# Weight loads moved to SyncE's queue, attention rows of four pairs moved to GpSimd, and a new instruction order, in a fused threshold attention and feed-forward kernel

## The chip, the cores and the metric

The kernel runs on one core of one Trainium2 chip. The core has five engines with instruction queues of their own: TensorE (PE; PEld is its weight load), VectorE (DVE), ScalarE (ACT), GpSimd (POOL) and SyncE (SP). Each works through its queue in order; engines wait for one another through semaphores. DMA transfers are issued by SyncE, ScalarE or GpSimd and carried out by 16 DMA engines that all of them share. The metric is the device time of one execution in microseconds, here the median of several runs.

## What is computed

Threshold attention over 8 batches and 8 heads, 576 tokens, 64 wide; its output, with the heads side by side, is the input of a feed-forward layer with a quick GELU.

```python
scores = scale * np.matmul(q, k.transpose(0, 1, 3, 2))
thresh = np.max(scores, axis=-1, keepdims=True) - tau
scores = np.where(scores >= thresh, scores, -1000000000.0)
scores = scores - np.max(scores, axis=-1, keepdims=True)
attn = np.exp(scores)
attn = attn / (np.sum(attn, axis=-1, keepdims=True) + 1e-09)
attn_out = np.matmul(attn, v).astype(np.float32)
x = np.ascontiguousarray(attn_out.transpose(0, 2, 1, 3)).reshape(B * S, H * D)   # 4608 x 512
h = x @ w_in                                     # 512 x 2048
g = h * (1.0 / (1.0 + np.exp(-1.702 * h)))
out = (g @ w_out).astype(np.float32)             # 2048 x 512
```

q, k and v are 32-bit floats. The two weight matrices come as 64-bit floats, and the kernel makes 32-bit ones of them on the chip.

## The kernel before

**Units of work.** Two heads make a pair: 32 pairs, four in each batch, numbered through. Tokens of the feed-forward part go in 18 blocks of 256 (`BLK`). A block needs all pairs of its tokens' batch.

**Stages.** The four pairs of batch 0 are worked "straight" (functions `straight_...`, lines 640 to 760): scores with queries on the partitions, row maximum on VectorE, threshold and exponential on ScalarE, transposes on TensorE (L699, L700), copies out of PSUM, then the product with v (L740) and the reciprocal sums (L746). All later pairs use transposed scores: `scores` (L531), `keep` (copies on ScalarE, L548), `in_groups` (group maxima and later group sums on VectorE, L554), a fold over the groups, `sub`, `mask`, `exps` and `values` (L767), and `place_x` (L859), which writes the block's input. The first two blocks use plain products: `mm1_0` (L917) and `mm2` (L896). Later blocks use `mm1` (L874) and a Strassen form of the second product, `product` (L1068), which needs sums of weight quarters; these come from `t_minus` (a negation on ScalarE) and `t_plus` (four accumulating DMAs of 1 MB issued by GpSimd, L1028). The last four blocks use a Strassen form of the first product as well (L982).

**Weights.** `load_w` (L455) brings 32 pieces of 128 x 512 numbers, 512 KB each, to staging places: unused quarters of `w_out`'s home and four places in `arena`, twelve in all. GpSimd issues them. `cv_ex`, `cv_frac`, `cv_join` and `cv_end` on VectorE (L463, L481, L488, L495) and `cv_power`, `cv_power2` on ScalarE (L470, L474) turn a piece into 32-bit numbers; `cv_end` frees its place. The first six pieces also wait for `hold` (L522), a one-column copy on GpSimd that reads pair 3's transposed k, so that no weight moves before the q and k of the four straight pairs are in.

**Loads and rows by SyncE.** `load_qk` (L392) and `load_v` (L406 for the straight pairs, L414 for the others) issue four DMAs for each tensor and pair, mostly through SyncE. The row of thresholds of a later pair has to reach all partitions: `row_out` (L604) writes it to DRAM in two DMAs, `row_in` (L613) waits for that and reads it back, broadcast, in two more. The reciprocal sums of pairs 4 and up go the same way by `sums_out` (L826) and `sums_in` (L833). All of these were issued by SyncE, as are the stores of results (L1095, L1098).

**Order.** The kernel is scheduled by hand. `task` enters a piece of work with an engine, an estimated duration, a rank, the pieces it comes after, and buffer places that it takes and gives. `run_in_order` then simulates all engines: whenever an engine is free, it starts the ready task of the lowest rank whose places are free, and the instructions are emitted in that order. So a rank sets which of several ready tasks goes first, and an estimated duration moves everything behind it. The rank of a task is its number (pair, or a line such as `W_RANK` for weights) plus a bias by its function's name from `EARLY` (pairs 0 to 3), `SECOND` (pairs 4 to 7), `LATER` or `CV` (weights). Feed-forward work on TensorE has the rank `LAST`. Two movers stand for DMA: "DMS" for transfers of SyncE, "DMW" for those of GpSimd; each takes its transfers in order, and while both are at work they share the rate by `SHARE`.

Of the kernel before, what the change touches and what calls it, by code (L numbers as in the profile page):

```python
# [10 lines left out]
FP32 = mybir.dt.float32  # L11
I32 = mybir.dt.int32
U32 = mybir.dt.uint32
# [6 lines left out]
P = 128  # L20
# [10 lines left out]
def kernel(  # L31
# [34 lines left out]
    nc = tc.nc  # L66
    B, H, S, D = q.shape
# [45 lines left out]
    flat = [const.tile([P, 32], FP32, name=f"flat{j}") for j in range(2)]  # L113
    flat_s = [const.tile([P, 32], FP32, name=f"flat_s{j}") for j in range(2)]
    gap = const.tile([P, 1], FP32, name="gap")
    stop = const.tile([P, 1], FP32, name="stop")
    eye = const.tile([P, P], FP32, name="eye")
    shift = const.tile([P, 1], FP32, name="shift")
    NQT = -(-S // P)
# [10 lines left out]
    for x in ("P0", "P1", "P2", "PT0", "PT1"):  # L130
        limits[x] = 1

    EARLY = {
        "load_qk": -6.99,
        "load_v": 19.38,
        "prep": -0.3,
        "straight_bias": -37.57,
        "straight_copy": 8.04,
        "straight_copy1": 11.5,
        "straight_exps": 20.62,  # L140
        "straight_mask": -13.68,
        "straight_max": -0.2,
        "straight_place": 8.36,
        "straight_rc": 12.79,
        "straight_scores": -8.82,
        "straight_spread": -20.84,
        "straight_turn": -58.57,
        "straight_values": -0.62,
        "w_sum": 90.41,
    }  # L150
    SECOND = {
        "exps": -8.01,
        "in_groups": 121.89,
        "keep": 8.52,
        "load_qk": -60.94,
        "load_v": 127.47,
        "mask": 92.02,
        "over_halves": -26.23,
        "over_tiles": -53.86,
        "place_x": -40.91,  # L160
        "prep": 109.09,
        "row_in": -38.28,
        "row_out": 19.96,
        "scores_run": -1.49,
        "sub": 24.27,
        "sums_in": 27.21,
        "sums_out": -40.63,
        "turn_rows": -31.38,
        "turn_sums": 97.65,
        "values": 117.99,  # L170
    }
    LATER = {
        "exps": 26.76,
        "in_groups": 140.58,
        "keep": -31.05,
        "load_qk": 105.64,
        "load_v": 65.31,
        "mask": 18.17,
        "over_halves": -22.78,
        "over_tiles": 5.19,  # L180
        "place_x": -61.68,
        "prep": -28.15,
        "row_in": -9.02,
        "row_out": 27.42,
        "scores_run": 19.47,
        "sub": 29.93,
        "sums_in": -9.33,
        "sums_out": 25.19,
        "turn_rows": -36.12,
        "turn_sums": -33.9,  # L190
        "values": -39.61,
        "x_sum": -32.27,
    }
    CV = {
        "cv_end": -7.74,
        "cv_ex": -36.17,
        "cv_frac": 2.14,
        "cv_join": -50.97,
        "cv_power": 117.41,
        "cv_power2": 87.54,  # L200
        "load_w": 4.35,
    }

    LAG = {"PE": 0.26, "DVE": 0.18, "ACT": 0.22, "POOL": 0.18, "SP": 0.1}
# [14 lines left out]
    FIRST, LAST = -9.0, 1000.0  # L219
    MOVERS = ("DMS", "DMW")  # L220

    SHARE = (0.22, 0.6)

    def moved(kind):
        pass
# [217 lines left out]
    def load_w(i):  # L443
        dst, src, c, j = pieces[i]
        dram = src[ts(c, P), ts(j, WC)]
        if not wide:
            nc.gpsimd.dma_start(out=dst[:, c, ts(j, WC)], in_=dram)
            return
        at = staged(i)
        if at in W64:  # L450
            t = arena[:, ts(W64.index(at), 2 * WC)]
        else:
            t = w_out[:, ts(HALVES.index(at), 2), :].rearrange("p a b -> p (a b)")
        t = t.bitcast(U32)
        nc.gpsimd.dma_start(out=t, in_=dram.bitcast(U32), max_dma_last_dim=1024)  # L455
        t = t.rearrange("p (c w) -> p c w", w=2)
        cv[i] = t[:, :, 1], t[:, :, 0], dst[:, c, ts(j, WC)]

# [38 lines left out]
        )  # L497


    held_k = {}  # L500
    mats, sT, stats, mbs, rows, pss = {}, {}, {}, {}, {}, {}

    def prep(n, which):

        dst, raw = home(n, f"qkT{which}"), raws.pop((n, which))
        if which and n < NPAIR:
            tiles = raw.rearrange("p (j k) -> p j k", k=KT)
            for u in range(2):
                nc.vector.transpose(
                    out=dst[:, 0 : 8 * KT].rearrange("p (x u k) -> p x u k", u=2, k=KT)[:, :, u],  # L510
                    in_=tiles[:, 5 * u : 5 * u + 4],
                )
            nc.vector.transpose(out=dst[:, 8 * KT :], in_=tiles[:, 4])
        else:
            nc.vector.transpose(out=dst, in_=raw)
        mats[n, which] = dst
        if which:
            held_k[n] = dst

    def hold(n):  # L520

        nc.gpsimd.tensor_copy(out=stop, in_=held_k[n][:, 0:1])  # L522

    def halves(ap):
        return ap.rearrange("p (c s) -> p c s", c=2)
# [72 lines left out]
        mbs[n] = mb  # L598


    def row_out(n):
        rows[n] = dram.tile([2, S], FP32, name="row", tag="row", bufs=2)
        for c in range(2):
            nc.sync.dma_start(  # L604
                out=rows[n][c : c + 1].rearrange("o (g i) -> (o g) i", i=32),
                in_=flat[1][ds(c * KT, QB)],
            )

    def row_in(n):
        mb = home(n, "mb")  # L610
        row = rows.pop(n)
        for c in range(2):
            nc.sync.dma_start(out=mb[ts(c, KT)], in_=row[c : c + 1].to_broadcast([KT, S]))  # L613
        mbs[n] = mb

    def sub(n, t):
# [206 lines left out]
    def sums_out(n):  # L823
        rcs[n] = dram.tile([2, 2, SH], FP32, name="row_s", tag="row_s", bufs=2)
        for c in range(2):
            nc.sync.dma_start(  # L826
                out=rcs[n][c].rearrange("h (g i) -> (h g) i", i=32), in_=flat_s[1][ds(c * KT, QB)]
            )

    def sums_in(n):  # L830
        rc, row = seat("rc"), rcs.pop(n)
        for h in range(2):
            nc.sync.dma_start(  # L833
                out=rc[ts(h, D)].rearrange("p (c s) -> p c s", c=2),
                in_=row[:, h].unsqueeze(0).to_broadcast([D, 2, SH]),
            )
        rcs[n] = rc
# [307 lines left out]
    BY_DMA = (0, 1, *range(3, NP))  # L1145
    SUMS_BY_DMA = range(4, NP)
    LEAD = 6
    WHOLE = 6

    FFU = 1.727  # L1150
    T_RANK = FIRST

    W_RANK = (-53.35, -5.67, 56.61, 61.89, -5.56, 48.51)
    W_TIME = 1.9
    ready_w, w_loads = [], []
    for i in range(len(pieces)):
        y = 0 if i < NDC else 2 if i < n_in else 4
# [4 lines left out]
            ready_w.append(task("POOL", 1.2, rank, load_w, i, lag=2.5))  # L1162
            continue
        place = (staged(i),)
        a = task("POOL", 0.6, rank, load_w, i, after=w_loads[-1:], take=place)
        w_loads.append(a)
        a = transfer("DMW", W_TIME, a)

        over = [
            ready_w[y] for y in range(i)  # L1170
# [220 lines left out]
        return transfer("DMS", 0.7 if n < NPAIR else 1.1, lv, 1)  # L1391

    HOLD = 3
    S_RANK = (-4.42, -17.19, 4.68)

    def straight(preps):
        order = [(n, t) for n in range(NPAIR) for t in range(2)]
# [5 lines left out]
        for u, (n, t) in enumerate(order):  # L1403
            r = S_RANK[0] * n if t < 2 else S_RANK[1] + S_RANK[2] * n
            whole, H = heads(t) == 2, range(heads(t))
            if t in (0, 2):
                lv = one_v(n, 1.0 + (0.5 * n if t == 0 else 1.6 + 0.6 * n))
            pt, pp = f"PT{u % 2}", f"P{p_of(n, t)}"
            a = task(
                "PE", 1.0 if whole else 0.6, r, straight_scores, n, t, after=preps[n] + chain[0][-1:],  # L1410
                take=("psA",) * heads(t) + (pp,), give=("s_m",) if t == NQT - 1 else (),
            )
            chain[0].append(a)
# [7 lines left out]
            if last_of[p_of(n, t)] == u:  # L1421
                back = ((pp,), ("mb", "rc"), ("s_t", "s_t"))[p_of(n, t)]
            a = task(
                "PE", 1.1 if whole else 0.55, r, straight_turn, n, t, after=es + chain[1][-1:],
                take=("psA", "psM"), give=back,
            )
            chain[1].append(a)
# [10 lines left out]
            new = n == 0 and t % 2 == 0  # L1438
            first = [spread_0[0, t // 2 * 2]] if not new else []
            a = task(  # L1440
                "PE", 1.31 if whole else 0.85, r, straight_values, n, t, after=c + [d, lv],
                give=(pt,) + ((f"v_m{n % 2}",) if t in (1, NQT - 1) else ()),
            )
            spread_0[n, t] = task(
# [10 lines left out]
    SPLIT = (True,)  # L1455
    preps = [load_pair(n, 0.5 * n, [], False) for n in range(NPAIR)]
    tasks[tau_done][5].extend(preps[0])
    h = task("POOL", 0.3, FIRST, hold, HOLD, after=preps[HOLD][1:])
    for a in w_loads[0:6]:
        tasks[a][5].append(h)  # L1460
    straight(preps)
    first_blocks()

    for n in range(NPAIR, NP):
# [3 lines left out]
        r = float(n)  # L1468

        slow = 1.1 if n < 2 * NPAIR else 1.0  # L1470
        behind = [spread[n - 2]] if n >= NPAIR + 2 else preps[-1]
        pq, pk = load_pair(n, r, behind, True)
        lv = one_v(n, r - 1.2)
        mx, copies = [], []

# [50 lines left out]
        )  # L1526
        if n in BY_DMA:
            a = task("DVE", 0.21, r, turn_rows, n, after=[a])
            a = transfer("DMS", 0.3, task("SP", 0.65, r, row_out, n, after=[a]))
            spread[n] = task("SP", 1.1, r, row_in, n, after=[a], take=("mb",))  # L1530
            m = transfer("DMS", 0.7, spread[n], 1, give=("row",))
        else:
            m = task("DVE", 0.78, r, spread_max, n, after=[a], take=("mb",))
        spread.setdefault(n, m)
# [21 lines left out]
        if n not in SUMS_BY_PE:  # L1556
            su = [
                task("DVE", 0.77 if t == NKT else 1.3, r, in_groups, n, t, ALU.add, after=[ws[t]])
                for t in range(NKT + 1)
            ]  # L1560
            a = task("DVE", 0.47, r, over_tiles, n, ALU.add, after=su + [pv], give=back)
            if n in SUMS_BY_DMA:
                a = task("DVE", 1.46, r, turn_sums, n, after=[a], take=("row_s",))
                a = transfer("DMS", 0.3, task("SP", 0.65, r, sums_out, n, after=[a]))
                a = task("SP", 1.2, r, sums_in, n, after=[a], take=("rc",))
                summed[n] = transfer("DMS", 0.7, a, 1, give=("row_s",))
            else:
                a = task("DVE", 1.6, r, one_group, n, after=[a])
        exped[n] = ws + su
# [40 lines left out]
```

## Time and profile before

| | us |
|---|---|
| median of 3 runs | 1312.84 (1311.53 to 1313.91) |
| the profiled execution, its own time | 1317.27 |
| its span, first to last instruction | 1315.5 |
| TensorE busy in the span | 1275.2 |
| VectorE busy | 987.2 |
| ScalarE busy | 675.9 |
| GpSimd busy | 241.8 |
| first `mm1_0` (L917) | at 72.11 |
| first `mm1` (L874), once pairs 4 to 7 are placed | at 283.80 |

DMA by queue, from the page:

```profile
q1 hardware_dynamic: 181456, 63.70, 20.4%
q0 software_dynamic: 8800, 20.97, 6.2%
```

q1 carries what SyncE issues (packets, MB, share of 16 engines over the span), q0 what GpSimd issues: the weights and the four accumulates.

How to read it: in the profile a line such as "L455 POOL" is line 455 of the kernel before on GpSimd; "SPq" is SyncE's queue of DMA issues. A row's duration there is how long the engine took to issue, not the transfer. "A <- B" in the view of waits means that A's engine stood idle until B. The busy time of TensorE has modelled ends, so a busy TensorE is not one at its peak. A stretch's DMA share can exceed 1 by a little, since packets overlap.

### The profile page before, as it was taken

Reading aid. Unit: us, or ns where it says so; the run is one execution under the profiler, and the core shown is the slowest. Engines: PE = TensorE matmul, PEld = TensorE weight load, DVE = VectorE, ACT = ScalarE, POOL = GpSimd, SP = SyncE. Lnnn points to the kernel's source line nnn. Section 1 sums busy time; section 2 is a strip of 40 time slices with the busy share of each in tenths; the row PEclk is TensorE's granted clock in tenths of the full one; section 3 lists DMA queues with packets and bytes.
Section 4 is the critical chain, followed back from the end, with each engine's and each line's share of the span. In section 5 each row is a group of like instructions: output and inputs, shape, how many; then the busy total and the mean of one; then the engine's idle time right before and its main releaser. Section 6 shows DMA issues by size and latency. Waiting matters only on the chain.

```text
span 1315.5 us, 22946 instructions
## 1 busy us (share of the span) xinstructions
PE 1275.2 (97%) x9140; PEld 994.8 (76%) x9140; DVE 987.2 (75%) x1648; ACT 675.9 (51%) x954; POOL 241.8 (18%) x265
## 2 busy tenths in 40 slices
PE   6599999899999999999999999999999999999998
PEld 4466764467887777777778887777777778888887
DVE  6698998998978888788787878777788863652642
ACT  6699965867745544555554555454555540210210
POOL 3001101013131211213021302021112117120120
PEclk9799999999999999999999999999999999999999
DMA  7724346364422222212222222222122110000000
GB/s 170 206 58 142 90 132 125 71 130 80 89 64 71 55 55 69 49 53 56 56 44 71 55 71 55 71 55 67 39 58 54 37 45 9 9 1 29 4 1 32
DMA packets 192730, 86.42 MB, mean 66 GB/s; under 512 B 159856, under 2 KB 173168, under 8 KB 192624
## 3 DMA queue, kind: packets, MB, share of 16 engines
q1 hardware_dynamic: 181456, 63.70, 20.4%
q0 software_dynamic: 8800, 20.97, 6.2%
q8 instruction: 71, 1.16, 0.4%
q10 hardware_dynamic: 2368, 0.30, 0.1%
q14 instruction: 35, 0.29, 0.1%
HBM read 71.04 MB, written 9.70 MB: 61 GB/s over the span
## 4 chain that ended last, share of the span: by engine, by line
PE 79%; DVE 6%; ACT 5%; DMA 4%; issue 3%; SPq 1%; POOL 0%; DVEq 0%; POOLq 0%; ACTq 0%
PE ops L1068 25%; PE hps L874 24%; PE pv L767 9%; PE ps L531 8%; PE ps L982 4%; PE ps L1068 4%; PE ops L982 3%; PE ops L896 2%; DVE arena L618 2%; ACT arena L628 1%; SPq L392 1%; DMA arena<-in_moe_w_in_dram 1%; ACT arena L624 1%; ACT arena L548 1%; DVE part L554 1%
## 5 line engine op out<-in xcount | busy, mean ns | idle before, releaser
L554 DVE TRANSPOSE_TENSOR_REDUCE part<-arena 128x36 f32<-128x1152 f32 (+1 forms) x280 | 338.2, 1234 | 43.8 <-ACT arena L548 24.0
L874 PE MATMUL hps<-xT,w_in 128*128 128x256 f32 x1536 | 336.7, 380 | 0.0
L874 PEld LDWEIGHTS hps<-xT,w_in 128*128 128x128 f32 x1536 | 290.8, 190 | 44.7 <-issue 5.7
L624 ACT ACTIVATE arena<-arena 128x1152 f32<-128x1152 f32 (+1 forms) x140 | 144.3, 1061 | 140.8 <-DVE arena L618 139.9
L1068 PE MATMUL ops<-w_out,arena 128*128 128x256 f32 x896 | 202.5, 380 | 0.9 <-DVE arena L886 0.8
L548 ACT COPY arena<-ps 128x576 f32<-128x576 f32 x252 | 150.4, 644 | 99.5 <-PE ps L531 97.8
L618 DVE TENSOR_TENSOR arena<-arena 128x1152 f32<-128x1152 f32 (+1 forms) x140 | 179.8, 1326 | 14.8 <-DMA arena<-row 14.8
L1068 PEld LDWEIGHTS ops<-w_out,arena 128*128 128x128 f32 x896 | 169.2, 190 | 28.3 <-DVE arena L886 2.7
L628 ACT ACTIVATE arena<-arena,shift,scl 128x1152 f32<-128x1152 f32 (+1 forms) x140 | 170.0, 1246 | 1.2
L1034 POOL TENSOR_TENSOR arena<-arena 128x256 f32<-128x256 f32 x56 | 52.0, 928 | 637.1 <-DVE arena L886 531.3
L531 PE MATMUL ps<-arena 64*64 64x288 f32 x2016 | 151.0, 408 | 6.3 <-ACT arena L548 4.9
L1068 PE MATMUL ops<-arena 128*128 128x256 f32 x672 | 150.6, 380 | 0.0
L883 ACT ACTIVATE th<-hps 128x512 f32<-128x512 f32 x112 | 66.5, 593 | 162.6 <-PE hps L874 153.5
L767 PE MATMUL pv<-arena 64*64 64x288 f32 x2016 | 147.3, 407 | 0.0
L1068 PEld LDWEIGHTS ops<-arena 128*128 128x128 f32 x672 | 127.3, 190 | 19.3 <-issue 2.2
L531 PEld LDWEIGHTS ps<-arena 64*64 64x64 f32 x2016 | 72.7, 133 | 58.1 <-ACT arena L548 16.8
L767 PEld LDWEIGHTS pv<-arena 64*64 64x64 f32 x2016 | 74.6, 134 | 51.2 <-issue 11.3
L1090 DVE SCALAR_TENSOR_TENSOR osb<-ops,osb 128x256 f32<-128x256 f32 x98 | 39.3, 413 | 93.8 <-PE ops L1068 87.5
L886 DVE SCALAR_TENSOR_TENSOR arena<-th,hps 128x512 f32<-128x512 f32 x96 | 64.5, 672 | 45.5 <-ACT th L883 45.3
L917 PE MATMUL hps<-xT,w_in 128*128 128x256 f32 x256 | 60.8, 387 | 3.4 <-DVE arena L923 2.4
L917 PEld LDWEIGHTS hps<-xT,w_in 128*128 128x128 f32 x256 | 46.8, 190 | 16.2 <-DVE arena L923 5.8
L1047 POOL TENSOR_TENSOR arena<-arena 128x512 f32<-128x512 f32 x28 | 38.1, 1363 | 113.1 <-PE ops L1068 113.1
(129 smaller groups left out, 1289.4 us busy)
## 6 DMA issues: line engine op xcount, KB each, us to landing
arena<-in_v_dram SPq DMA_DIRECT2D x112, 144.0 KB
arena<-in_q_dram SPq DMA_DIRECT2D x128, 72.0 KB
out_dram<-osb SPq DMA_DIRECT2D x36, 256.0 KB
arena<-in_k_dram SPq DMA_DIRECT2D x124, 72.0 KB
arena<-row SPq DMA_DIRECT2D x56, 144.0 KB
arena<-row_s SPq DMA_DIRECT2D x56, 144.0 KB
w_out<-in_moe_w_in_dram POOLq DMA_DIRECT2D x12, 512.0 KB, 9.2
arena<-in_moe_w_out_dram POOLq DMA_DIRECT2D x12, 512.0 KB, 5.2
```

The lines of the kernel that those rows point to most:

```text
L531: nc.tensor.matmul(ps[ts(c, KT), h, 0:SH], lhsT=mats[n, 1][ts(h, D), ts(j, KT)], rhs=mats[n, 0][ts(h, D), ts(c, SH)], start=True, stop=True,)
L548: nc.scalar.copy(out=sT[n, t][:, u], in_=pss.pop((n, j))[:, :, 0:SH])
L554: nc.vector.tensor_reduce(out=stats[n, op][:, t * 2 * QB : min(2 * t + 2, NK) * QB], in_=sT[n, t].rearrange("p u h (g d) -> p (u h g) d", ...
L618: nc.vector.tensor_tensor(out=s, in0=s, in1=mbs[n].unsqueeze(1).to_broadcast(list(s.shape)), op=ALU.subtract)
L624: nc.scalar.activation(out=s, in_=s, func=AF.Prelu, alpha=STEEP)
L628: nc.scalar.activation(out=s, in_=s, func=AF.Exp, scale=scl, bias=shift)
L767: nc.tensor.matmul(o[c][ts(h, D), 0:SH], lhsT=left(j, h)[ts(c, KT)], rhs=sT[n, t][ts(c, KT), u, h, :], start=(j == 0), stop=(j == NK - 1),)
L874: nc.tensor.matmul(hidden[j][:, ts(f, BLK)], lhsT=w_in[:, c, ds((f * HF + j) * P, P)], rhs=xTs[blk][:, c, :], start=(c == 0), stop=(c == N ...
L883: nc.scalar.activation(out=ths[j], in_=hidden[j], func=AF.Tanh, scale=GELU_SCALE / 2)
L917: nc.tensor.matmul(hidden[j // 2][:, ts(j % 2, BLK)], lhsT=w_in[:, c, ts(j, P)], rhs=xTs[i][:, c, :], start=(c == 0), stop=(c == NDC - 1),)
L982: nc.tensor.matmul(places[j, x], lhsT=left[:, c, ts(j, P)], rhs=right[:, c, :], start=(c == 0), stop=(c == 1),)
L1068: nc.tensor.matmul(banks[blk][k][:, ts(o, HM)], lhsT=left[:, j, :], rhs=right[:, j, :], start=(j == 0), stop=(j == HF - 1),)
```

## The change

1. `load_w` is issued by SyncE, without the limit of 1024 elements for a DMA's last dimension; its transfers join those of q, k and v in "DMS", as a third kind with a share of its own. Its task is on SyncE at 0.65 us, and a transfer is taken as 1.6 us, not 1.9. `hold`, its tile and its wait are taken out.
2. `row_out`, `row_in`, `sums_out` and `sums_in` go through `row_queue`: GpSimd for the pairs in `ROWS_BY_POOL` (0 to 7; pairs 0 to 3 have no such rows), SyncE for the others. The planner gives them 1.4 times SyncE's cost, the mover "DMW" and a lag of 2.2 us.
3. The loads of q and k of pair 4 and up come after `prep` of the pair before, and after `row_in` of the pair two before only where SyncE issues that.
4. All biases, `W_RANK` and `S_RANK` have new values, and the TensorE tasks of the straight pairs longer estimated durations.

The diff, with the rank tables cut to the entries of loads, rows and a few others:

```diff
-    stop = const.tile([P, 1], FP32, name="stop")
...
     EARLY = {
-        "load_qk": -6.99,
-        "load_v": 19.38,
-        "prep": -0.3,
+        "load_qk": 3.05,
+        "load_v": 82.62,
+        "prep": 362.76,
...
     SECOND = {
-        "in_groups": 121.89,
-        "load_qk": -60.94,
-        "load_v": 127.47,
-        "mask": 92.02,
+        "in_groups": 369.01,
+        "load_qk": -36.91,
+        "load_v": 29.17,
+        "mask": 366.05,
...
     LATER = {
-        "load_qk": 105.64,
-        "load_v": 65.31,
+        "load_qk": 2.64,
+        "load_v": -33.93,
...
     CV = {
-        "cv_power": 117.41,
-        "load_w": 4.35,
+        "cv_power": 390.1,
+        "load_w": 50.41,
...
-    SHARE = (0.22, 0.6)
+    SHARE = (0.15, 0.5, 0.6)
...
-        nc.gpsimd.dma_start(out=t, in_=dram.bitcast(U32), max_dma_last_dim=1024)
+        nc.sync.dma_start(out=t, in_=dram.bitcast(U32))
...
-        if which:
-            held_k[n] = dst
-
-    def hold(n):
-
-        nc.gpsimd.tensor_copy(out=stop, in_=held_k[n][:, 0:1])
...
+    def row_queue(n):
+        return nc.gpsimd if n in ROWS_BY_POOL else nc.sync
+
     def row_out(n):
         rows[n] = dram.tile([2, S], FP32, name="row", tag="row", bufs=2)
         for c in range(2):
-            nc.sync.dma_start(
+            row_queue(n).dma_start(
...
+    ROWS_BY_POOL = range(8)
...
-    W_RANK = (-53.35, -5.67, 56.61, 61.89, -5.56, 48.51)
-    W_TIME = 1.9
+    W_RANK = (-4.5, 72.77, 54.26, 75.15, 32.14, 155.99)
+    W_TIME = 1.6
...
-        a = task("POOL", 0.6, rank, load_w, i, after=w_loads[-1:], take=place)
+        a = task("SP", 0.65, rank, load_w, i, after=w_loads[-1:], take=place)
         w_loads.append(a)
-        a = transfer("DMW", W_TIME, a)
+        a = transfer("DMS", W_TIME, a, 2)
...
-    S_RANK = (-4.42, -17.19, 4.68)
+    S_RANK = (0.4, 5.42, 2.97)
...
-                "PE", 1.0 if whole else 0.6, r, straight_scores, n, t, after=preps[n] + chain[0][-1:],
+                "PE", 1.13 if whole else 0.78, r, straight_scores, n, t, after=preps[n] + chain[0][-1:],
...
-                "PE", 1.1 if whole else 0.55, r, straight_turn, n, t, after=es + chain[1][-1:],
+                "PE", 1.2 if whole else 0.64, r, straight_turn, n, t, after=es + chain[1][-1:],
...
-                "PE", 1.31 if whole else 0.85, r, straight_values, n, t, after=c + [d, lv],
+                "PE", 1.43 if whole else 0.87, r, straight_values, n, t, after=c + [d, lv],
...
-    h = task("POOL", 0.3, FIRST, hold, HOLD, after=preps[HOLD][1:])
-    for a in w_loads[0:6]:
-        tasks[a][5].append(h)
...
-        behind = [spread[n - 2]] if n >= NPAIR + 2 else preps[-1]
+        rq = ("POOL", 1.4, "DMW", 2.2) if n in ROWS_BY_POOL else ("SP", 1.0, "DMS", 1.7)
+        behind = preps[n - 1] + ([spread[n - 2]] if n - 2 >= NPAIR and n - 2 not in ROWS_BY_POOL else [])
         pq, pk = load_pair(n, r, behind, True)
+        preps.append([pq, pk])
...
-            a = transfer("DMS", 0.3, task("SP", 0.65, r, row_out, n, after=[a]))
-            spread[n] = task("SP", 1.1, r, row_in, n, after=[a], take=("mb",))
-            m = transfer("DMS", 0.7, spread[n], 1, give=("row",))
+            a = transfer(rq[2], 0.3, task(rq[0], 0.65 * rq[1], r, row_out, n, after=[a]))
+            spread[n] = task(rq[0], 1.1 * rq[1], r, row_in, n, after=[a], take=("mb",))
+            m = transfer(rq[2], 0.7, spread[n], 1, give=("row",), lag=rq[3])
```

`sums_out` and `sums_in` are edited like `row_out` and `row_in`.

More of the change, by code (lines that the diff above doesn't have):

```diff
@@ L133 @@
     EARLY = {
-        "load_qk": -6.99,
-        "load_v": 19.38,
-        "prep": -0.3,
[L137 to L149, printed above, removed]
+        "load_qk": 3.05,
@@ L150 @@
+        "load_v": 82.62,
+        "prep": 362.76,
+        "straight_bias": -51.59,
+        "straight_copy": -11.87,
+        "straight_copy1": -4.39,
+        "straight_exps": 57.8,
+        "straight_mask": -49.11,
+        "straight_max": -16.77,
+        "straight_place": 30.11,
+        "straight_rc": 32.02,
+        "straight_scores": 63.84,
+        "straight_spread": 5.07,
+        "straight_turn": 64.19,
+        "straight_values": -79.72,
+        "w_sum": 48.82,
     }
     SECOND = {
-        "exps": -8.01,
@@ L153 @@
-        "in_groups": 121.89,
-        "keep": 8.52,
-        "load_qk": -60.94,
-        "load_v": 127.47,
-        "mask": 92.02,
[L158 to L170, printed above, removed]
+        "exps": 53.23,
@@ L171 @@
+        "in_groups": 369.01,
+        "keep": -16.96,
+        "load_qk": -36.91,
+        "load_v": 29.17,
+        "mask": 366.05,
+        "over_halves": 54.1,
+        "over_tiles": 97.84,
+        "place_x": 12.39,
+        "prep": 32.35,
+        "row_in": 55.92,
+        "row_out": 8.7,
+        "scores_run": -21.91,
+        "sub": 17.15,
+        "sums_in": 5.03,
+        "sums_out": -4.82,
+        "turn_rows": 155.43,
+        "turn_sums": 9.77,
+        "values": -69.26,
     }
     LATER = {
-        "exps": 26.76,
@@ L174 @@
-        "in_groups": 140.58,
-        "keep": -31.05,
-        "load_qk": 105.64,
-        "load_v": 65.31,
[L178 to L192, printed above, removed]
+        "exps": 72.34,
@@ new lines @@
+        "in_groups": 363.35,
+        "keep": -33.06,
+        "load_qk": 2.64,
+        "load_v": -33.93,
+        "mask": -0.83,
+        "over_halves": -15.8,
+        "over_tiles": -22.38,
+        "place_x": -59.37,
+        "prep": 51.26,
+        "row_in": 156.1,
+        "row_out": -51.91,
+        "scores_run": 76.83,
+        "sub": 28.89,
+        "sums_in": 32.66,
+        "sums_out": 58.7,
+        "turn_rows": -35.09,
+        "turn_sums": 2.88,
+        "values": -15.13,
+        "x_sum": -24.18,
@@ L193 @@
     }
     CV = {
[L195 to L198, printed above, removed]
-        "cv_power": 117.41,
-        "cv_power2": 87.54,
-        "load_w": 4.35,
+        "cv_end": -5.82,
+        "cv_ex": 67.45,
+        "cv_frac": 58.08,
+        "cv_join": 17.15,
+        "cv_power": 390.1,
+        "cv_power2": 61.04,
+        "load_w": 50.41,
     }
@@ L497, in cv_end @@
         )
-    held_k = {}
     mats, sT, stats, mbs, rows, pss = {}, {}, {}, {}, {}, {}
@@ L612, in row_in @@
         for c in range(2):
-            nc.sync.dma_start(out=mb[ts(c, KT)], in_=row[c : c + 1].to_broadcast([KT, S]))
+            row_queue(n).dma_start(out=mb[ts(c, KT)], in_=row[c : c + 1].to_broadcast([KT, S]))
         mbs[n] = mb
@@ L825, in sums_out @@
         for c in range(2):
-            nc.sync.dma_start(
+            row_queue(n).dma_start(
                 out=rcs[n][c].rearrange("h (g i) -> (h g) i", i=32), in_=flat_s[1][ds(c * KT, QB)]
@@ L832, in sums_in @@
         for h in range(2):
-            nc.sync.dma_start(
+            row_queue(n).dma_start(
                 out=rc[ts(h, D)].rearrange("p (c s) -> p c s", c=2),
@@ L1563 @@
                 a = task("DVE", 1.46, r, turn_sums, n, after=[a], take=("row_s",))
-                a = transfer("DMS", 0.3, task("SP", 0.65, r, sums_out, n, after=[a]))
-                a = task("SP", 1.2, r, sums_in, n, after=[a], take=("rc",))
-                summed[n] = transfer("DMS", 0.7, a, 1, give=("row_s",))
+                a = transfer(rq[2], 0.3, task(rq[0], 0.65 * rq[1], r, sums_out, n, after=[a]))
+                a = task(rq[0], 1.2 * rq[1], r, sums_in, n, after=[a], take=("rc",))
+                summed[n] = transfer(rq[2], 0.7, a, 1, give=("row_s",), lag=rq[3])
             else:
```

## The prediction

> **What bounds the kernel now.** I began with the page: TensorE's share, and the span in 40 slices of 32.9 us.
>
> ```profile
> PE 1275.2 (97%) x9140; PEld 994.8 (76%) x9140; DVE 987.2 (75%) x1648; ACT 675.9 (51%) x954; POOL 241.8 (18%) x265
> ...
> PE   6599999899999999999999999999999999999998
> ...
> ACT  6699965867745544555554555454555540210210
> ```
>
> TensorE is full from the third slice on; only the first two, and a digit of the eighth, have room. The view of busy time by stretch puts numbers on that (stretch, its length, then PE, PEld, DVE, ACT, POOL, granted clock, DMA share, GB/s).
>
> ```profile
> 8.00:48.60 40.60, 32.32 (x284) 21.00 (x284) 34.13 (x92) 33.80 (x64) 10.60 (x15) 0.92 0.90 240
> 48.60:55.70 7.10, 0.00 (x0) 0.00 (x0) 0.00 (x0) 0.00 (x0) 0.75 (x1) 0.60 0.73 172
> 55.70:66.00 10.30, 9.33 (x90) 7.93 (x94) 5.62 (x16) 6.57 (x14) 0.00 (x0) 0.78 0.17 45
> 66.00:165.00 99.00, 95.17 (x953) 68.73 (x946) 87.37 (x187) 96.70 (x178) 9.73 (x13) 1.00 0.36 98
> 165.00:195.00 30.00, 27.61 (x171) 20.47 (x171) 28.40 (x51) 19.58 (x30) 2.25 (x3) 1.00 0.52 140
> 195.00:284.00 89.00, 84.09 (x561) 40.46 (x561) 80.28 (x124) 56.62 (x68) 3.92 (x3) 0.98 0.47 99
> 284.00:1088.00 804.00, 803.66 (x6057) 640.49 (x6056) 647.43 (x982) 433.42 (x546) 158.53 (x163) 1.00 0.26 60
> ```
>
> From 284 us TensorE is busy 803.66 of 804: a fixed amount of matmul work, so whatever the beginning gains or loses, the end gains or loses. From 66 to 165 ScalarE is the bound (96.70 of 99), from 165 to 195 VectorE (28.40 of 30), and TensorE again from 195. Ahead of them lies a hole, 48.6 to 55.7, in which no engine computes. The timeline of SyncE's issues and the waits say why.
>
> ```profile
> 24.25 11.10 SPq L392 DMA_DIRECT2D arena<-in_q_dram  x4
> 35.45 14.80 SPq L392 DMA_DIRECT2D arena<-in_k_dram  x4
> 50.34 22.55 SPq L406 DMA_DIRECT2D arena<-in_v_dram  x16
> PE rest L740 <- DMA arena<-in_v_dram: 10.3, 1, 10.3
> ```
>
> Four loads of q, which took 2.27 us to issue at 8.96, take 11.10 at 24.25, and four of k take 14.80 instead of 2.67. Behind them in SyncE's order stands the next v, issued at 50.34, for which TensorE waits 10.3 us. What slows them is the other queue:
>
> ```profile
> 28.00:32.00 4.00, 3.91 (x44) 2.89 (x44) 3.44 (x10) 3.91 (x9) 1.07 (x2) 1.00 1.02 325
> 32.00:36.00 4.00, 4.00 (x60) 2.79 (x56) 3.97 (x9) 3.97 (x8) 2.01 (x3) 1.00 1.05 340
> ```
>
> The DMA engines are full (share 1.02 to 1.05) with the 512 KB weight pieces that GpSimd issued from 21.6 us on.
>
> **The change, part by part.** (1) *Weights to SyncE.* One queue means that q and k no longer share the engines with weights packet by packet; they take their turn. A piece moves in 0.524 MB / 0.340 MB per us = 1.54 us. No weight issue by SyncE is in the trace: the nearest rows are a 256 KB store, 0.37 us, and one of four q loads, 2.27 / 4 = 0.57. 32 pieces take 12 to 18 us of SyncE, spread over some 180 us. The gain is the hole, 55.7 - 48.6 = 7.1 us, and the low granted clock (0.60 and 0.78 in the two rows) around it: the two batches of twenty L740 matmuls with their L746 last from 55.7 to 60.9, 5.2 us, against 3.9 from 24.0 to 27.8: 1.3. Together 8.4. Two bounds. Another wait may come right behind (gain 0); or everything comes, at most TensorE's whole 10.3 us wait. I take 8.4, because ScalarE and VectorE are idle there too, and ScalarE, the bound of the next 99 us, gets that much more time.
>
> (2) *Weights ahead of the first v.* Ranks order what SyncE has ready: pieces 0 and 1 (-4.5 + 50.41 = 45.9, then 65.2) go ahead of v of pairs 0 and 1 (1.0 + 82.62 = 83.6, 84.1). That costs the first v 2 x (0.37 to 0.57) of issue up to 2 x 1.54 of transfer, 0.7 to 3.1 us. The first L740 (23.97) moves with it; the scores and exps of the next tiles, which ScalarE works on until then, cover it in part. I take 1; without that cover it is 3.1. Taking out `hold` and the GpSimd copy (0.18 us) costs nothing: GpSimd sat idle 18.9 us there.
>
> (3) *Rows of pairs 4 to 7 by GpSimd.* Each pair has two `row_out`, two `row_in`, two `sums_out`, two `sums_in`: 8 DMAs, 32 in all. On GpSimd a DMA takes 0.75 us (the L455 row), so 24 us, against some 14 on SyncE (0.31, 0.49, 0.31 and 0.61 us). GpSimd is idle 27.75 of the 30 us after 165, so the issuing itself is hidden. The latency is not, always: SyncE's first row goes out at 119.64 and `row_in`, which waits for it, starts at 121.47, 1.83 us. GpSimd's tau load landed 3.4 us after issue, and its quickest weight piece in 4.0, less 1.54 of transfer 2.5. So a hop costs +0.6 to +1.6, four hops a pair +2.4 to +6.4. VectorE has other pairs to work on meanwhile (80.28 of 89); exposed is the last pair, whose sums go out at 264.9 and whose chain has to end before the first L874 at 283.8. Against it stands a gain: SyncE's rows stood among other issues, and the chain of waits has these.
>
> ```profile
> 162.15 8.15 DMA row_s<-flat_s
> ...
> 220.23 2.85 DMA row<-flat
> 223.65 7.40 DMA arena<-row
> ```
>
> 7.40 us came beside a 1 MB accumulate and eight q and k loads, and ended in TensorE's wait of 4.91 us on ScalarE at 250. If it goes, the gain is that 4.91; if GpSimd's latency is exposed in full, the cost is 6.4. GpSimd works in order too: a row can now stand behind an accumulate that waits for ScalarE's negation (9.0 us before the one at 207.3), and the accumulate behind a row; that makes the upper end 9.0. I take 0, because VectorE waits only 3.8 us for `row` and 3.0 for `row_s` from 60 to 285.
>
> The Trainium skill has a rule against this part: "SBUF — State Buffer", section "SBUF: two separate sides", says that DMAs issued by GpSimd stall while VectorE holds the port that both share, since their descriptors can't be written; it gives 620 ns alone and 3100 ns overlapped. By the page a hop would be 2.5 us longer and a pair 9.9. In the trace the L455 issue stays at 751 to 782 ns with VectorE nearly full, so the issue shows no such stall; landings of 4.0 to 13.8 us could hide one.
>
> (4) *New ranks, and longer TensorE costs for the planner.* They add no instruction; they change the order on every engine. TensorE's idle time outside the hole and the first 8 us, up to 284, is 8.28 (8 to 48.6) + 0.97 + 3.83 + 2.39 + 4.91, less 3.2 (its 10.3 less the 7.1 inside the hole): 17.2. At best all of that goes, at worst a second hole of 10.3 opens. I take 0, by the nearest row: ScalarE at 96.70 of 99 says that this idle time is mostly TensorE waiting for a full engine, which no order removes. The low priority of `prep` (362.76) and of `in_groups` (369.01) costs nothing as long as VectorE has gaps early (34.13 busy of 40.6). From 284 on, order moves nothing: TensorE is full.
>
> The sum: -8.4 + 1 + 0 + 0 = -7.4. The profiled execution took 1317.27 (span 1315.5 and 1.8 around it), so 1309.9 for it; it lies 4.4 above the median of the runs, 1312.84, so 1305.4 for the median: 1305.
>
> **Rivals.** *A: a v load that waits holds the weights* (slower). SyncE works in order. In the trace it stands for TensorE to free a v seat: L406 on L746 three times, 24.2 us, the longest 17.0; L414 on L740 27.6 us at once. Meanwhile GpSimd went on issuing weights (96.34 to 108.10, 130.88, 132.08, 156.47 to 159.28). After the change these are behind it, wherever the real order runs later than the planned one. One w_in piece held 17.0 us holds the first product as long: 1312.8 + 17.0 - 8.4 = 1321. It decides from a hold of 8.4 us on. Against it: the planner lets SyncE take a v only when its seat is free in its own time, and other pieces are in hand.
>
> *B: the hole moves.* The bytes are the same. If the v of pair 2 queues behind twelve pieces, 12 x 1.54 = 18.5 us of transfer from about 22 to 40 and SyncE is held as before, nothing is gained: 1313. For it: q, k, v and weights fill the engines from 24 to 48. Against: ranks put v of pairs 2 and 3 (84.6, 85.1) ahead of piece 3 (103.9) and later ones, and TensorE needed it only at 45.4. The Trainium skill's "DMA: Bandwidth & Descriptors", section "Issuing engines are not separate DMA queues", is on B's side: all issuers interleave on the same 16 engines and only sequencer time is saved. The trace differs: 11.10 against 2.27 us is what sharing did to q.
>
> *C: GpSimd's latency comes to lie on the chain.* If the beginning ends 8.4 earlier, pair 7's slack (its sums landed near 270.5, mm1 at 283.8: 13) is only 5; with hops at the longest lone landing, 6.08 - 1.54 = 4.5, +2.7 each and +10.8 a pair, in pair 7 and, through SyncE's queue order, once more in pair 6 on the way to 231: -8.4 + 1 + (10.8 - 5) + 4.5 = +2.9, 1316. Against it: VectorE has other work at each hop. The Trainium skill's rule in part 3 speaks for C.
>
> **How the numbers follow.** Forecast 0.55, A 0.20, B 0.13, C 0.12. A measurement tells 0.2%, 2.6 us, from no change. The forecast, whose own range is 1294 to 1311, is faster in 0.53 and the same in 0.02; A slower in 0.20; B faster in 0.03, the same in 0.06, slower in 0.04; C faster in 0.02, the same in 0.03, slower in 0.07. Sums: faster 0.58, same 0.11, slower 0.31. The range goes from 1305 - 17 = 1288 (all idle time of part 4 gone) to A's 1321 with 2 more for part 2 uncovered.
>
> **What would show it.** Right: no stretch over 3 us between 30 and 70 us without computing; q and k of pair 4 issued in some 3 us each; the first L917 (now 72.11) and the first L874 (283.80) some 7 us earlier; ScalarE still full in between. Part 3: 2.4 to 3.4 us from `row_out` to `row_in`. Wrong: weight issues right behind an L406 or L414 that stands over 8 us (A); v of pair 2 after 45 us again (B); VectorE or TensorE waiting for `row` or `row_s` by over 5 us in all before 284 (C); or a new idle stretch that none of these names, made by the order.

## The result and the profile after

The changed kernel takes 1312.56 us (median of 20 runs, 1308.09 to 1316.72) against 1315.41 of the kernel before, measured beside it (20 runs). The ratio is 0.9978, interval 0.9968 to 0.9988: faster by 2.9 us, where 7.4 had been forecast. (The forecast of 1305 started from 1312.84, the median of the first three of these 20 runs of the kernel before; from 1315.41 it would have been 1308.) The two profiled executions lie 5.1 us apart (1312.18 and 1317.27); that of the kernel before was 1.9 above its median, so the traces overstate the difference by some 2 us.

Busy time by stretch, changed kernel, over the stretches that were shown of before (then PE, PEld, DVE, ACT, POOL, granted clock, DMA share, GB/s):

```profile
8.00:48.60 40.60, 32.07 (x306) 20.43 (x306) 31.90 (x82) 30.59 (x59) 0.00 (x0) 0.92 0.76 164
48.60:55.70 7.10, 6.57 (x78) 4.16 (x78) 5.79 (x12) 6.99 (x13) 0.00 (x0) 1.00 0.71 202
55.70:66.00 10.30, 6.21 (x46) 4.18 (x43) 8.06 (x22) 6.16 (x14) 0.00 (x0) 0.68 1.01 367
66.00:165.00 99.00, 94.39 (x910) 70.42 (x909) 87.10 (x188) 93.90 (x173) 2.28 (x5) 1.00 0.34 99
165.00:195.00 30.00, 29.53 (x174) 21.04 (x173) 28.46 (x50) 22.36 (x31) 4.20 (x8) 1.00 0.45 138
195.00:284.00 89.00, 86.33 (x582) 43.98 (x581) 77.87 (x122) 56.68 (x72) 15.92 (x23) 0.98 0.46 102
284.00:1088.00 804.00, 802.37 (x6050) 639.08 (x6048) 647.77 (x982) 428.51 (x541) 162.72 (x166) 1.00 0.25 60
```

The hole is gone: TensorE, VectorE and ScalarE work from 48.6 to 55.7. TensorE is busy 802.37 of the last 804 us shown (803.66 before), so the beginning still decides nearly all. But the stretch behind the old hole is now poor, with ScalarE busy 6.16 of 10.3 and TensorE 6.21, at a granted clock of 0.68, while the DMA engines are full. From 66 to 165 ScalarE has 5.1 us idle, where it had 2.3.

The views of waits name the new stall, the whole span for TensorE and then 8 to 290 us for all engines:

```profile
PE ps L654 <- DVE arena L507: 8.7, 1, 8.7
PE ps L654 <- ACT arena L675: 7.3, 3, 4.1
PE rest L735 <- DMA arena<-in_v_dram: 2.3, 1, 2.3
```

```profile
ACT arena L675 <- DVE stat L669: 16.2, 3, 11.1
DVE w_in L462 <- DMA w_out<-in_moe_w_in_dram: 5.7, 5, 1.9
```

The wait for v has shrunk from 10.3 to 2.3 us; one of up to 4.1 on ScalarE has appeared. (ScalarE's 11.1 and TensorE's 8.7 are the start of the kernel, as before.) The timeline shows its root (start, duration, what; idle time before it in brackets):

```profile
54.41 2.56 SPq L454 DMA_DIRECT2D w_out<-in_moe_w_in_dram  x3
...
58.67 0.43 DVE L462 TENSOR_SCALAR w_in<-w_out 128x512 int32<-128x512 int32 x1 [1.93 <-DMA w_out<-in_moe_w_in_dram]
...
59.47 0.75 DVE L664 TENSOR_REDUCE stat<-ps 128x1 f32<-128x576 f32 x1
...
60.57 0.74 ACT L675 ACTIVATE arena<-ps,stat 128x576 f32<-128x576 f32 x1 [3.65 <-DVE stat L669]
...
61.36 1.70 PE L654 MATMUL ps<-arena 64*64 64x288 f32 x10 [4.09 <-ACT arena L675]
```

VectorE works in order and stands at `cv_ex` (L462) for a weight piece that hasn't landed. The row maximum (L664) of a straight pair is queued behind it, ScalarE waits for that maximum, and TensorE for ScalarE. The pieces are late because of what SyncE does before them:

```profile
26.85 2.97 SPq L391 DMA_DIRECT2D arena<-in_q_dram  x4
29.92 2.71 SPq L391 DMA_DIRECT2D arena<-in_k_dram  x4
...
38.62 4.27 SPq L391 DMA_DIRECT2D arena<-in_q_dram  x4
42.99 4.60 SPq L391 DMA_DIRECT2D arena<-in_k_dram  x4
47.68 2.51 SPq L405 DMA_DIRECT2D arena<-in_v_dram  x4
50.24 2.33 SPq L454 DMA_DIRECT2D w_out<-in_moe_w_in_dram  x4
```

Pair 4's q and k now issue in 5.7 us, not 25.9. But at 38.62 come q and k of pair 5, 8.9 us of issue, and only at 50.24 the next nine weight pieces. VectorE transposes pair 5's q and k (L513) at 106.73, 59 us after they are issued.

### The profile page after: what moved, and what is told of

It is laid out like the page before. It is cut to its first block, busy times and chain, and to the rows that moved or that the text cites. A ratio compares the mean times of both kernels' runs of the same rounds, so it can differ in the third digit from the quotient of the medians.

```text
span 1310.4 us, 22945 instructions
## 1 busy us (share of the span) xinstructions
PE 1275.4 (97%) x9140; PEld 994.7 (76%) x9140; DVE 984.7 (75%) x1648; ACT 673.7 (51%) x954; POOL 236.1 (18%) x264
## 4 chain that ended last, share of the span: by engine, by line
PE 80%; DVE 8%; ACT 5%; DMA 4%; SPq 1%; issue 1%; POOL 0%; DVEq 0%; POOLq 0%
PE ops L1063 26%; PE hps L869 23%; PE pv L762 9%; PE ps L523 9%; PE ps L977 4%; PE ps L1063 4%; PE ops L977 3%; DVE arena L613 2%; SPq L391 1%; DVE part L546 1%; ACT arena L683 1%; PE hps L912 1%; ACT arena L675 1%; PE ops L891 1%; DMA row<-flat 1%
## 5 line engine op out<-in xcount | busy, mean ns | idle before, releaser
L869 PE MATMUL hps<-xT,w_in 128*128 128x256 f32 x1536 | 337.2, 380 | 0.6 <-DVE arena L881 0.5
L869 PEld LDWEIGHTS hps<-xT,w_in 128*128 128x128 f32 x1536 | 290.7, 190 | 46.0 <-issue 5.3
L540 ACT COPY arena<-ps 128x576 f32<-128x576 f32 x252 | 149.4, 644 | 97.4 <-PE ps L523 96.6
L1085 DVE SCALAR_TENSOR_TENSOR osb<-ops,osb 128x256 f32<-128x256 f32 x98 | 39.4, 413 | 95.5 <-PE ops L1063 89.3
L1042 POOL TENSOR_TENSOR arena<-arena 128x512 f32<-128x512 f32 x28 | 38.4, 1374 | 110.5 <-PE ops L1063 110.3
L997 ACT ACTIVATE th<-arena 128x512 f32<-128x512 f32 x32 | 20.2, 630 | 72.7 <-DVE arena L993 72.7
```

The costliest lines, as they stand in the source:

```text
L540: nc.scalar.copy(out=sT[n, t][:, u], in_=pss.pop((n, j))[:, :, 0:SH])
L869: nc.tensor.matmul(hidden[j][:, ts(f, BLK)], lhsT=w_in[:, c, ds((f * HF + j) * P, P)], rhs=xTs[blk][:, c, :], start=(c == 0), stop=(c == N ...
```

## The experiments

To separate queues from order, nearly all experiments keep a kernel's planned order and change only which engine issues a DMA, or where in SyncE's queue one stands. All compute the whole reference. A move is written like this in `run_in_order`, here for e1; the others differ in the two conditions:

```diff
-                tasks[i][3](*tasks[i][4])
+                f, a = tasks[i][3], tasks[i][4]
+                if f is load_qk and a[0] == 4:
+                    kept.append((f, a))
+                    continue
+                f(*a)
+                if f is load_v and a[0] == 3 and kept:
+                    for f, a in kept:
+                        f(*a)
+                    kept.clear()
```

**e1: the kernel before, pair 4's q and k behind v of pair 3.**

> The kernel before with one move: the q and k loads of pair 4 are issued by SyncE right after the v of pair 3, not ahead of the v of pair 2; nothing else changes. It measures the term of the prediction that the hole (7.1 us, 8.4 with the low clock) was worth. Theory (the hole's worth is carried through to the end, the change lost it elsewhere): some 8 us faster than before, about 1307. Rival (a hole in the beginning is given back by ScalarE and VectorE later): at most 4 us faster, 1311 or more.

Measured: 1304.50 against 1316.27, ratio 0.9912 (0.9900 to 0.9925): 11.6 us faster, with eight DMAs moved. The granted clock stays at 1.00:

```profile
8.00:48.60 40.60, 34.04 (x340) 21.67 (x344) 33.53 (x93) 35.04 (x67) 10.87 (x16) 1.00 0.90 246
48.60:55.70 7.10, 5.80 (x56) 3.65 (x48) 6.93 (x19) 7.10 (x16) 0.65 (x1) 1.00 0.94 184
55.70:66.00 10.30, 10.30 (x118) 8.38 (x115) 9.98 (x28) 10.09 (x22) 0.75 (x1) 1.00 0.34 96
```

ScalarE is at work 10.09 of the 10.3 us in which it had 6.57. The first product starts at 59.9 (72.1 before), the second at 182.8 (194.7): twelve us early are carried from the start to the end. The rival, that they are given back on the way, falls. The hole was worth more than the 8.4 of the prediction.

**e2: the changed kernel, pair 5's q and k behind weight piece 13.** Conditions: `f is load_qk and a[0] == 5`, and `f is load_w and a[0] == 13`.

> The changed kernel with the q and k loads of pair 5 issued after weight piece 13, not between pieces 5 and 6; prep of pair 5 runs some 50 us later in any case. Theory (in the one queue these loads hold eight weight pieces back, VectorE stands for two of them and ScalarE and TensorE for some 4 us around 57 to 61 us): that stall goes, 3 to 4.5 us faster than the changed kernel, 1308 to 1309.5. Rival (the new order, not the queue, costs the time; the first product is 10 us later in it in any case): within 1 us of the changed kernel, 1312 to 1313.5.

Measured: 1309.53, ratio to before 0.9942 (0.9929 to 0.9956), so 4.7 us faster than the changed kernel. The stretch that was poor:

```profile
55.70:66.00 10.30, 8.04 (x96) 5.64 (x94) 9.92 (x28) 9.95 (x21) 0.00 (x0) 1.00 0.72 164
```

ScalarE 9.95 instead of 6.16, clock 1.00 instead of 0.68. The theory holds.

**e3: the changed kernel, weight pieces 0 and 1 behind v of pairs 0 and 1.** Conditions: `f is load_w and a[0] < 2`, and `f is load_v and a[0] == 1 and kept`.

> The changed kernel with weight pieces 0 and 1 issued after the v of pairs 0 and 1, not ahead of them. Theory (the first v 2.8 us late, TensorE waiting 2.3 us for it and running at a granted clock of 0.5 behind it, is a loss carried through): 1.5 to 2.5 us faster than the changed kernel, 1310 to 1311. Rival (ScalarE's work covers it): within 1 us of it.

Measured: 1312.84, ratio 0.9973 (0.9964 to 0.9982). The changed kernel's 0.9978 is inside, so the gain isn't told from nothing, though the first product with v moved from 26.8 to 24.4. The theory's gain did not come, but the run doesn't show that a late v is free, because its trace has a new stall in place of the old one:

```profile
29.42 0.43 DVE L471 TENSOR_SCALAR w_in<-w_out 128x512 int32<-128x512 int32 x1 [6.56 <-DMA w_out<-in_moe_w_in_dram]
...
35.47 2.19 PE L663 MATMUL ps<-arena 64*64 64x288 f32 x12 [7.60 <-ACT arena L684]
```

Piece 0 is now late. VectorE stands 6.56 us for it, because its own order is that of the changed kernel, with row maxima queued behind the conversion, and TensorE stands 7.60 us for ScalarE. The stretch from 55.7 to 66 is full in this run (ScalarE 9.95 of 10.3) with pair 5's loads in the same place: TensorE had lost its time earlier.

**e4: the changed kernel with its rows issued by SyncE.**

```diff
-        return nc.gpsimd if n in ROWS_BY_POOL else nc.sync
+        return nc.sync
```

> The changed kernel, in the same order, with the rows of pairs 4 to 7 issued by SyncE again. Theory (rows on GpSimd cost nothing that is exposed): within 1.5 us of the changed kernel, or slower by up to 5 where a row now stands behind a weight that waits for its place on SyncE. Rival (GpSimd's longer hops are on the chain and ate the gain): 2 to 4 us faster, 1308.5 to 1310.5.

Measured: 1314.64, ratio 0.9985 (0.9976 to 0.9994): within a us of the changed kernel. In the new order the queue of the rows makes no difference that can be told.

**e5: the kernel before with weights issued by SyncE, its own order.**

```diff
-        nc.gpsimd.dma_start(out=t, in_=dram.bitcast(U32), max_dma_last_dim=1024)
+        nc.sync.dma_start(out=t, in_=dram.bitcast(U32))
```

> The kernel before, in its own order, with the weights issued by SyncE: part 1 of the change alone, with no new rank and no row moved. Six weight pieces now stand between the q and k loads of pair 4 and nine ahead of the v of pair 2. Theory (what counts is which load stands ahead of which v; the second queue matters little): part of the hole stays, since the v of pair 2 lands behind some 14 us of weights and 3.6 us of q and k: 3 to 9 us faster than before. Rival (sharing between two queues is the cost, and one queue removes it): the full 12 us of e1, 1304.

Measured: 1308.11, ratio 0.9938 (0.9926 to 0.9950): 8.2 us faster, as the theory had it and short of the rival's 12. TensorE's wait for v is 2.0 us in this run.

**e6: e1 and e5 together.**

> e1 (before, pair 4's q and k behind the v of pair 3) with the weights issued by SyncE too. Theory: one queue adds nothing to e1 and may cost a little, since nine weight pieces stand ahead of the v of pair 2 and later weights behind v loads that wait for their place: 1304.5 to 1310. Rival (one queue is a gain of its own): faster than e1 by over 2 us, under 1302.5.

Measured: 1306.39, ratio 0.9922 (0.9910 to 0.9935). Not told apart from e1: with the loads in the right order, one queue or two is the same within some 2 us.

**e7: e6 with the rows of pairs 4 to 7 issued by GpSimd.**

> e6 with the rows of pairs 4 to 7 issued by GpSimd: both moves of queues that the change makes, in the order before, with pair 4's q and k late. Theory: rows on GpSimd are neutral when the weights have left its queue: within 2 us of e6. Rival (longer hops are exposed): 3 to 6 us slower than e6.

Measured: 1308.44, ratio 0.9944 (0.9932 to 0.9955), 2.9 us slower than e6; the intervals overlap only at their ends. That lies between theory and rival. In e6 TensorE waits 4.5 us, at the scores of L540, for copies of earlier scores; in e7 the same wait is 7.6.

**e8: the changed kernel with its weights issued by GpSimd.**

> The changed kernel, in its order, with the weights issued by GpSimd again (limit of 1024 elements back, the first two pieces behind a copy of pair 3's transposed k, as before). GpSimd then runs twelve pieces ahead against the q, k and v of pairs 4, 2, 5 and 3 on SyncE. Theory (SyncE's loads are stretched as in the kernel before, v of pair 2 behind q and k of pair 4): 3 to 8 us slower than the changed kernel, 1315 to 1320. Rival (the queue is of no account, the order alone sets the time): within 1.5 us of it.

Measured: 1325.44, ratio 1.0068 (1.0056 to 1.0080): slower than the changed kernel by 11.8 us, more than the theory had, and slower than the kernel before. SyncE's loads are stretched again:

```profile
23.98 9.22 SPq L401 DMA_DIRECT2D arena<-in_q_dram  x4
33.31 16.47 SPq L401 DMA_DIRECT2D arena<-in_k_dram  x4
49.88 2.62 SPq L415 DMA_DIRECT2D arena<-in_v_dram  x4
```

**e9: the kernel before with both moves of queues and no new rank** (e5 and the rows of pairs 4 to 7 by GpSimd).

> The kernel before in its own order with both moves of queues and no new rank: weights by SyncE (e5) and rows of pairs 4 to 7 by GpSimd. With the changed kernel it isolates the new ranks. Theory (the new order itself is a loss of some 3 us here and 6 with rows on SyncE; rows on GpSimd cost some 3 in an order that was not made for them, as between e6 and e7): 1310 to 1312, 4 to 6 us faster than before, and 1 to 3 us faster than the changed kernel. Rival (the new order is neutral or a gain once the rows are on GpSimd): as slow as the changed kernel or slower, 1312.5 and more.

Measured: 1310.28 against 1315.25, ratio 0.9954 (0.9942 to 0.9967): 6.1 us faster than before, and 3.2 faster than the changed kernel, whose interval begins at 0.9968.

**e10: e1 with pair 4's q and k later still** (after the second v of pair 1).

> e1 with pair 4's q and k later still: after the second v of pair 1, still ahead of their use. Theory (what counts is that v and weights of the straight pairs are not behind loads that are used 40 us later): as fast as e1 or up to 2 us faster, 1302 to 1305. Rival (they then come too late for pair 4 and its scores stand): slower than e1 by over 1 us, 1305.5 and more.

Measured: 1304.87, ratio 0.9920 (0.9908 to 0.9932): as e1. They aren't late there either. e1, e10 and e6 aren't told apart; all three are faster than both kernels.

## Why the prediction was wrong in size

The ratios, times 1316 us, give each part of the change alone:

| step | from, to | predicted us | measured us |
|---|---|---|---|
| (1) weights to SyncE | before, e5 | -8.4 | -8.2 |
| (3) rows to GpSimd | e5, e9 | 0 (-4.9 to +9.0) | +2.1 |
| (2) and (4) new order: ranks, costs, what loads come after | e9, after | +1 + 0 (-17.2 to +10.3) | +3.2 |
| sum | | -7.4 | -2.9 |

The first measured step carries some 1.6 us either way, the others, differences of two measurements, some 2. Of (3) the intervals of e5 and e9 overlap, of (4) those of e9 and after don't. Of the 4.5 us that are missing, 2.1 are in (3), within the noise, and 2.2 in (2) and (4) together, where e2 says what happened.

**What bounds it** was right. TensorE is all but full from 284 us on, and e1's twelve us arrive at the end.

**Step (1)** was right in sign and size for this change. That the hole alone was worth 8.4 was too low: e1 takes 11.6 out (9.9 to 13.2). Part of that is the term for the low clock. Its measure, the batches from 24.0 to 27.8 (3.9 us), ran at a granted clock of 0.50 themselves until 26; two such batches take 2.8 us at 1.00 in the changed kernel (38.4 to 41.2), so the term is 2.4 and not 1.3. One queue gets 8.2 of it (e5); q and k of pair 4 and nine weight pieces still stand ahead of v of pair 2 there, for which TensorE waits 2.0 us. The mechanism was half right: "What slows them is the other queue" is true of the trace, but e1 keeps that queue and loses the hole. What cost the time was q and k of pair 4, issued from 24 us on and first used for scores at 89.4, standing in front of v.

**Step (2)**, +1, stays unmeasured. TensorE's wait of 2.3 us is exposed on the spot, but e3 removes it only at the price of another stall, so no run tells what of it reaches the end.

**Step (3)**, 0: +2.1 in the old order, -0.9 in the new (e4). Hops from first `row_out` to `row_in` on GpSimd, read from its timeline in the changed kernel, and of `sums_out` to `sums_in` likewise, are 2.4 to 3.0 us in five cases, as predicted (2.4 to 3.4), and 5.0, 5.9 and 7.9 in three. The two longest:

```profile
164.86 1.02 POOL L821 DMA_DIRECT2D row_s<-flat_s  x2 [44.95 <-DVE flat_s L816]
170.79 1.25 POOL L828 DMA_DIRECT2D arena<-row_s  x2 [4.92 <-DMA row_s<-flat_s]
...
211.25 1.63 POOL L1023 DMA_DIRECT2D arena<-w_out  x1 [7.14 <-DVE w_out L494]
214.21 1.10 POOL L599 DMA_DIRECT2D row<-flat  x2 [1.32 <-DVE flat L583]
222.09 1.07 POOL L608 DMA_DIRECT2D arena<-row  x2 [6.78 <-DMA row<-flat]
```

The one at 214 was issued right behind an accumulate of GpSimd, the one at 165 right behind two weight pieces of SyncE (163.78 and 164.25); that these delayed them is likely, not shown. So the gain that part 3 allowed for, the 8.15 and 7.40 us of the old chain, did not come: the new chain has 4.86 and 7.60 in their places. The stall of GpSimd's DMAs under VectorE that the Trainium skill describes ("SBUF — State Buffer", "SBUF: two separate sides") doesn't show in the issues: the sixteen `row` and `row_s` writes take 505 to 570 ns each on GpSimd, ten of them from 195 to 284, where VectorE is busy 77.87 of 89 us. Ten of the sixteen land within 2.6 us; the other six, 3.8 to 7.6, could hide one.

**Step (4) failed**: "They add no instruction; they change the order on every engine ... I take 0". The bound was there ("at worst a second hole of 10.3 opens"), the choice was wrong. It was argued from ScalarE's row alone, and the order of SyncE's queue was read only as far as the first v and the ranks of later ones. Read further, it has q and k of pair 5 ahead of weights that VectorE needs at once. The kernel has one place for a later pair's q and one for its k (`raw0`, `raw1`), which `prep` frees. The rank of `prep` for pairs 4 to 7 was lowered:

```diff
     SECOND = {
...
-        "prep": 109.09,
+        "prep": 32.35,
```

So pair 4 is transposed some 50 us earlier (the kernel before, then the changed one), and pair 5's loads, whose rank is low in both kernels (-60.94 and -36.91), go out at 38.62 instead of 87.86:

```profile
87.07 0.77 DVE L515 STREAM_TRANSPOSE arena<-arena 128x576 f32<-128x576 f32 x1
...
36.27 1.43 DVE L513 STREAM_TRANSPOSE arena<-arena 128x576 f32<-128x576 f32 x2
```

e2 moves just these eight DMAs and gains 4.7 us, and then (0.9942) stands no worse than the old order with the same queues (e9, 0.9954, overlapping): this one place is enough to account for step (4)'s loss. That the rank of `prep` put them there is read from the code and the trace; no run changes that rank alone. The late first product is no mark of the loss: 7 us earlier was expected and 10.5 later came (82.6 against 72.1), but in e2, with the loss gone, it still starts at 79.5. The changed kernel's first L869 came 6.5 earlier all the same (277.3).

**The rivals.** A, weights held behind another load, came true only in kind: not behind a v that waits for its place, but behind q and k ahead of their use, and for 4, not 17 us. One v load does wait 13.8 us for its place, ahead of the weight piece at 99.90, but that piece then waits 10.5 more for a place of its own. B did not come: v of pair 2 issues at 33.42. The Trainium skill's "DMA: Bandwidth & Descriptors", "Issuing engines are not separate DMA queues", has the DMAs of all issuers interleave on the same engines, with only sequencer time to be saved by a second one. e1 against e6 agrees with it: one queue or two isn't told apart there. By itself it is not enough: with the order kept, the issuer of the weights makes 8.2 us in the kernel before (e5) and 11.8 in the changed one (e8), where GpSimd puts out eight pieces from 22.7 to 28.6 us and six more by 39.4, beside SyncE's q and k. C stays open: rows on GpSimd cost 2.1 (e5 to e9) and 2.9 us (e6 to e7) in the old order, the first within the noise and the second at its edge, and nothing in the new (e4). Its sign tells nothing: from 60 to 284 us VectorE waits 7.0 us for `row` and `row_s` after and 6.8 before.

## What to carry to other kernels

In a queue that works in order, look at every load for when it is used, not only for when it can go: q and k fetched some 40 to 60 us early cost 11.6 us in one kernel and 4.7 in the other, and moving them beat the whole change. When an order and a queue change together, measure them apart, by emitting one plan through the other's queues. An engine's own waits for DMA belong to its order: a conversion that can wait, placed ahead of a maximum that others need, stopped three engines, and e3 only moved that stop to another place.

## What the runs showed of the hardware that was not expected

SyncE's issue of a DMA gets longer when transfers stand ahead of it: a 512 KB piece takes 0.33 us at the shortest and 1.44 at the longest in the changed kernel, four q loads 1.94 at the shortest, 4.27 behind three pieces in the same queue and, in the kernel before, 11.10 beside GpSimd's. GpSimd issues a row's DMA in 0.51 to 0.65 us, less than the 0.75 of a weight piece that the prediction took. TensorE's granted clock can fall without any long wait. It was 0.50 from 28 to 32 us in the changed kernel after a wait of 2.3 us. But it was also 0.50 from 22.7 to 26.0 and from 39.8 to 43.1 in the kernel before, where TensorE had not waited over 1.05 us since its first matmul, and 1.00 from 8 to 66 us in e1, with waits of up to 1.3. What makes it fall isn't shown, and neither is what it costs at the end: e10 has both of these dips and isn't told apart from e1.
